# Closing the attention's pools and the first eight steps put into the attention's region of fixed order

## Chip, cores and metric

One core of a Trainium2 chip. The metric is the device time of one execution in microseconds (us); lower is better. Engines: TensorE (PE, its weight loads PEld), VectorE (DVE), ScalarE (ACT), GpSimd (POOL), and SyncE (SP), which issues the loads here.

## Reference

Three stages one behind the other, all in float32. A decaying linear attention over B=2, H=8, S=768, D=64 gives x (1536 x 512). It feeds two layers with d_ff = 2048, the first with an ELU, the second with a softplus.

```python
for b in range(nb):
    intra = einsum('bhic,bhjc->bhij', qb, kb) * Dmask
    intra = einsum('bhij,bhjd->bhid', intra, vb)
    inter = einsum('bhid,bhde->bhie', qb * lam_pow, kv_state)
    out[:, :, sl] = intra + inter
    kv_state = lam_block * kv_state + einsum('bhsd,bhse->bhde', kb * rev_pow, vb)
x = out as (tokens, heads * dim)
h = x @ w_in;   g = where(h > 0, h, exp(min(h, 0)) - 1);          x = g @ w_out
h = x @ w_in2;  g = maximum(h, 0) + log1p(exp(-abs(h)));          return g @ w_out2
```

## The kernel before

**Attention.** It runs over 12 chunks g of 128 tokens (6 for each of the two batches; state is carried inside a batch). For each chunk:
- S(g) is the scores on PE (att_s, L306, 8 matmuls a pair of banks, 16 rows in the trace), then the mask sc(g) on DVE (att_mask, L319, two instructions).
- X(g) is the chunk's output on PE (att_x): the part with the carried state first (L334, needs state(g-1) and the queries that POOL has scaled, L265), then the part inside the chunk (L343, needs sc(g)).
- T(g) is the state's product on PE (L370; it needs the keys that ACT, L284, and POOL, L291, have scaled). state(g) is formed from it on DVE (L376), and its decayed copy on POOL (L380).
- xh(g) on ACT (L357) and xl(g) on DVE (L358) split the chunk's output into a high and a low part, which the layers' matmuls read.

The program's order inside the loop is S(g+1), sc(g+1), scaling of chunk g+1, X(g), T(g), state(g), xh and xl(g). So PE has S(g+1) to do while the state of the chunk before is formed. Chunks 5 and 11 end a batch: they form no state, and chunk 6 needs none. There is no S(12).

**Weights.** Each weight is split on the chip into a high part wh and a low part wl. For the first five blocks fc of 128 rows this is done in halves (fc, i): i=0 for the first product, i=1 for the second. Such a half takes five steps (split_half), each on an in-order engine:
1. convert: two ACT instructions, r (L111) and c (L112), which read the loaded tile raw
2. shift: DVE, L116
3. round_up: DVE, L122
4. high: ACT, L125, writes wh
5. rest: DVE, L128, writes wl

The table PIECES lays the steps of (0, 0) and (1, 0) into chunks 5 to 11 of the attention: (1, 0) is converted behind chunk 8, shifted in chunk 9, rounded and made high in chunk 10, and its rest stands in chunk 11. The half (2, 0) and the later ones belong to early_step (table HALVES): (2, 0) to step 0, all five of its steps behind m1(0).

**Loads.** All loads but the constants go through SP's queue in the order of the table LOADS; the load of (2, 0) stands behind the last loads of the attention.

**Layers.** A step n is m1(n) on PE (12 matmuls of 128x512, L407 to L409), ACT's two instructions on its result (L418, L419), DVE's (L442), ACT's high part of g (L447), POOL's low part (L449), and two steps later m2(n-2) on PE (12 matmuls, L480). m1(0) needs (0, 0) and xh, xl of the first four chunks; m1(1) needs (1, 0); m1(2) needs (2, 0). The second loop of steps, from step 8, is unchanged by the diff.

**Order.** Inside `tc.manual_schedule()` every engine keeps the program's order. The kernel before has three such regions: the attention, steps 0 to 7, and (for all engines but DVE) the rest. Between the first two stands the closing of the attention's pools. Across two regions the scheduler may interleave.

```python
    with tc.manual_schedule():
        attention()
    close_attention()
    with tc.manual_schedule():
        for n in range(8):
            (early_step if n in HALVES else step)(n)
```

Of the kernel before, what the change touches and what calls it, by code (L numbers as in the profile page):

```python
# [48 lines left out]
def body(ctx, tc, consts, attqk, attkv, w1, w2, out):  # L49
# [480 lines left out]
    def close_attention():  # L530
        actx.close()
        late["acc"] = ctx.enter_context(tc.tile_pool(name="late", bufs=1, reuse_waits="tile"))
        late["tp"] = ctx.enter_context(tc.tile_pool(name="ltp", bufs=2, reuse_waits="tile"))
# [5 lines left out]
    def attention():  # L539
        setup()  # L540
        powers()
        decays()
        att_s(0)
        att_prep_k(0, att_turn_k())
        att_mask(0)
        for g in range(NCHUNK):
            before, behind = PIECES.get(g, ((), ()))
            att_s(g + 1)
            att_mask(g + 1)
            att_prep(g + 1)  # L550
            att_prep_k2(g + 1)
            if before:
                half(*before, 1 if g in (6, 9) else 2)
            ps = att_x(g)
            att_state(g)
            att_conv(g, ps)
            att_prep_k(g + 1)
            if behind:
                half(*behind, 1)
            loads(g or None)  # L560
# [43 lines left out]

    with tc.manual_schedule():
        attention()
    close_attention()
    with tc.manual_schedule():
        for n in range(8):
            (early_step if n in HALVES else step)(n)  # L610
    with tc.manual_schedule(engines={ET.PE, ET.Activation, ET.Pool, ET.SP}):
# [51 lines left out]
```

## Time and profile before

| what | value |
|---|---|
| time, median of 3 runs | 578.88 us (578.66 to 579.36) |
| profiled execution: its own time | 575.07 us |
| profiled execution: span of the core | 573.3 us |
| granted TensorE clock, mean | 0.999 |
| busy: PE / ACT / DVE / POOL | 563.6 / 361.3 / 341.7 / 165.3 us |

In the lists of instructions in order of time, a row gives start (us from the span's start), length (us), engine, line, operation, out<-in and, in brackets, how long the engine had stood idle before it and what ended that. One row can hold several instructions of a kind (x16); its length then runs from the first's start to the last's end. Matmuls are pipelined, so a row can begin a little before the row ahead of it ends.

### The profile page before, as it was taken

The page shows a single profiled execution, that of the slowest core. Times are in us where ns is not written, and L with a number is a line of the kernel's source. Part 1 is how long each engine was busy: PE and PEld are TensorE (multiplying, and loading weights), DVE is VectorE, ACT ScalarE, POOL GpSimd, SP SyncE. Part 2 cuts the span into 40 slices and gives each one's busy share as a digit, 9 for nine tenths or more (in the row PEclk, how much of TensorE's full clock was granted, in tenths as well). Part 3 has the DMA queues.
Part 4 walks back from the last instruction along what each step waited for, and adds up shares of the span by engine and source line. Part 5 has one row for each costly group of instructions (what it writes and reads, how often), then busy time and mean ns, then how long its engine had stood idle before and what let it go on. Part 6 is the DMA issues. An engine that isn't in the chain of part 4 may idle for free.

```text
span 573.3 us, 7779 instructions
## 1 busy us (share of the span) xinstructions
PE 563.6 (98%) x3031; PEld 468.6 (82%) x3031; DVE 341.7 (60%) x407; ACT 361.3 (63%) x597; POOL 165.3 (29%) x143
## 2 busy tenths in 40 slices
PE   9979999999999999999999999999999999999997
PEld 8867888888888888888888888888888888888885
DVE  6776644645454445113666967675799855656656
ACT  5566666666565654432877877756899755665562
POOL 4662221221222212432432452221221222222210
PEclk9999999999999999999999999999999999999999
DMA  8990321313322312000323202010241000100202
GB/s 334 408 405 19 147 74 74 146 74 105 117 74 90 131 73 74 0 2 0 120 109 141 73 1 73 18 57 1 74 148 73 2 0 1 73 1 0 74 0 75
DMA packets 10693, 49.60 MB, mean 87 GB/s; under 512 B 1184, under 2 KB 1568, under 8 KB 7072
## 3 DMA queue, kind: packets, MB, share of 16 engines
q1 hardware_dynamic: 10368, 48.89, 22.8%
q8 instruction: 24, 0.39, 0.3%
q10 hardware_dynamic: 288, 0.20, 0.1%
q14 instruction: 13, 0.11, 0.1%
HBM read 45.95 MB, written 3.15 MB: 86 GB/s over the span
## 4 chain that ended last, share of the span: by engine, by line
PE 91%; DMA 6%; DVE 1%; issue 0%; ACT 0%; SPq 0%; DVEq 0%; ACTq 0%
PE y L480 45%; PE hps L407 15%; PE hps L408 15%; PE hps L409 15%; DMA raw<-w 4%; DMA early<-attkv 2%; DMA kv<-attkv 1%; DVE yacc L527 0%; DVE sc L319 0%; PE xps L343 0%; SPq L250 0%; DVE state L376 0%; DVE c L122 0%; DVE yacc L482 0%; PE xps L334 0%
## 5 line engine op out<-in xcount | busy, mean ns | idle before, releaser
L407 PE MATMUL hps<-xh,wh 128*128 128x512 f32 x384 | 149.5, 389 | 0.0
L409 PE MATMUL hps<-xh,wl 128*128 128x512 f32 x384 | 149.5, 389 | 0.0
L408 PE MATMUL hps<-xl,wh 128*128 128x512 f32 x384 | 149.4, 389 | 0.0
L449 POOL TENSOR_TENSOR g<-v,g 128x512 fp32r<-128x512 f32 x48 | 62.9, 1310 | 193.1 <-ACT g L447 193.1
L480 PE MATMUL y<-g,wh 128*128 128x512 f32 x384 | 118.3, 389 | 0.0
L480 PE MATMUL y<-wh,g 128*128 128x512 f32 x382 | 117.7, 389 | 0.0
L449 POOL TENSOR_TENSOR g<-l,g 128x512 fp32r<-128x512 f32 x46 | 60.1, 1306 | 183.6 <-ACT g L447 164.2
L418 ACT ACTIVATE v<-hps 128x512 f32<-128x512 f32 x48 | 28.7, 598 | 100.4 <-PE hps L409 100.3
L442 DVE SCALAR_TENSOR_TENSOR v<-v,hps 128x512 f32<-128x512 f32 x48 | 32.9, 686 | 93.0 <-ACT v L419 92.8
L409 PEld LDWEIGHTS hps<-xh,wl 128*128 128x128 f32 x384 | 72.0, 188 | 15.1 <-DVE wl L128 0.2
L407 PEld LDWEIGHTS hps<-xh,wh 128*128 128x128 f32 x384 | 72.0, 188 | 15.1 <-issue 0.2
L408 PEld LDWEIGHTS hps<-xl,wh 128*128 128x128 f32 x384 | 72.1, 188 | 14.9
L480 PEld LDWEIGHTS y<-g,wh 128*128 128x128 f32 x384 | 72.1, 188 | 14.9
L480 PEld LDWEIGHTS y<-wh,g 128*128 128x128 f32 x382 | 71.7, 188 | 15.3 <-POOL g L449 0.2
L444 DVE TENSOR_TENSOR l<-l,u 128x512 f32<-128x512 f32 x48 | 75.6, 1574 | 4.4
L436 DVE SCALAR_TENSOR_TENSOR u<-u,e 128x512 f32<-128x512 f32 x48 | 33.6, 700 | 69.4 <-ACT l L430 69.4
L480 PE MATMUL y<-g,wl 128*128 128x512 f32 x192 | 74.7, 389 | 0.0
L480 PE MATMUL y<-wl,g 128*128 128x512 f32 x191 | 74.3, 389 | 0.0
L427 ACT ACTIVATE e<-hps 128x512 f32<-128x512 f32 x48 | 28.7, 598 | 71.2 <-PE hps L409 71.2
L128 DVE TENSOR_TENSOR wl<-c,wh 128x1024 fp32r<-128x1024 f32 (+1 forms) x36 | 50.0, 1389 | 14.4 <-ACT wh L125 14.0
L122 DVE CUSTOM_DVE_ANT_0 c<-r,c 128x2048 uint16<-128x2048 uint16 (+1 forms) x36 | 40.7, 1130 | 4.7 <-ACT c L112 1.8
L480 PEld LDWEIGHTS y<-g,wl 128*128 128x128 f32 x192 | 36.0, 188 | 7.6
(70 smaller groups left out, 605.7 us busy)
## 6 DMA issues: line engine op xcount, KB each, us to landing
raw<-w SPq DMA_DIRECT2D x28, 1024.0 KB, 4.8
early<-attkv SPq DMA_DIRECT2D x8, 512.0 KB, 10.2
raw<-w SPq DMA_DIRECT2D x8, 512.0 KB, 10.2
qk<-attqk SPq DMA_DIRECT2D x6, 512.0 KB, 8.1
early<-attqk SPq DMA_DIRECT2D x6, 512.0 KB, 10.8
out<-yacc SPq DMA_DIRECT2D x7, 256.0 KB, 2.0
kv<-attkv SPq DMA_DIRECT2D x3, 512.0 KB, 10.2
out<-o SPq DMA_DIRECT2D x4, 256.0 KB, 2.3
```

Of the source, the lines that this page charges most:

```text
L122: V.tensor_tensor(out=c, in0=r.bitcast(U32), in1=c, op=ALU.add)
L128: V.tensor_tensor(out=lo, in0=c.bitcast(F32), in1=hi.bitcast(F32), op=ALU.subtract)
L407: T.matmul(ps, wh[fc, 0][:, o], h[:, k, :], start=(k == 0), stop=False)
L408: T.matmul(ps, wh[fc, 0][:, o], l[:, k, :], start=False, stop=False)
L409: T.matmul(ps, wl[fc, 0][:, o], h[:, k, :], start=False, stop=(k == KD - 1))
L418: A.activation(out=v, in_=ps, func=AF.Relu, scale=-1.0)
L427: A.activation(out=e, in_=ps, func=AF.Abs)
L436: V.scalar_tensor_tensor(out=u, in0=u, scalar=-1.0, in1=e, op0=ALU.add, op1=ALU.subtract)
L442: V.scalar_tensor_tensor(out=v, in0=v, scalar=-1.0, in1=ps, op0=ALU.add, op1=ALU.max)
L444: V.tensor_tensor(out=v, in0=v, in1=u[0], op=ALU.subtract)
L449: eng.tensor_tensor(out=g[:, 1], in0=v, in1=g[:, 0].bitcast(F32), op=ALU.subtract)
L480: T.matmul(yps[m], a, b, start=(c == begin and i == 0), stop=(last and i == 2))
```

## The change

The two regions become one, with the closing of the pools inside it. No instruction is added or taken away; no size, tile or load changes.

```diff
     with tc.manual_schedule():
         attention()
-    close_attention()
-    with tc.manual_schedule():
+        close_attention()
         for n in range(8):
             (early_step if n in HALVES else step)(n)
```

What it moves is one half's split. On ACT, at the end of the attention, before the change (raw_133 and wh_757 are of the half (1, 0), raw and wh_847 of (2, 0); L357 is xh of the chunks, L284 the scaling of chunk 10's keys, L418 the first instruction on m1(0)'s result):

```order
L111 ACTIVATE r<-raw_133 128x512
L112 ACTIVATE c<-raw_133 128x512
L111 ACTIVATE r<-raw 128x512
L112 ACTIVATE c<-raw 128x512
L125 ACTIVATE wh_847<-r 128x512
L357 ACTIVATE xh_669<-xps 128x2x128 x2
L284 ACTIVATE early<-early,kdecay 128x64 x4
L125 ACTIVATE wh_757<-r 128x512
L357 ACTIVATE xh_669<-xps 128x2x128 x4
L418 ACTIVATE v<-hps 128x512
```

The same place with the change (wh_844 is now the high part of (2, 0)):

```order
L111 ACTIVATE r<-raw_133 128x512
L112 ACTIVATE c<-raw_133 128x512
L357 ACTIVATE xh_669<-xps 128x2x128 x2
L284 ACTIVATE early<-early,kdecay 128x64 x4
L125 ACTIVATE wh_757<-r 128x512
L357 ACTIVATE xh_669<-xps 128x2x128 x4
L111 ACTIVATE r<-raw 128x512
L112 ACTIVATE c<-raw 128x512
L125 ACTIVATE wh_844<-r 128x512
L418 ACTIVATE v<-hps 128x512
```

The three ACT instructions of (2, 0) stood ahead of xh(9), and now stand behind xh(11), the attention's last.

On DVE at the same place, before the change (wl_848 is the low part of (2, 0), wl_758 that of (1, 0); the first row holds the shifts of both halves, (1, 0) first; the three L358 rows are xl of chunks 9, 10 and 11, the two L376 rows state(9) and state(10), the L319 rows sc(11)):

```order
L116 TENSOR_SCALAR r<-r 128x512 x2
L122 ISA c<-r,c 128x1024
L376 TENSOR_TENSOR state<-stps,faded 128x256
L358 TENSOR_TENSOR xl_670<-xps,xh_669 128x2x128 x2
L128 TENSOR_TENSOR wl_848<-c,wh_847 128x512
L319 TENSOR_TENSOR sc<-sps_742,dmask 128x512
L319 TENSOR_TENSOR sc<-sps_743,dmask 128x512
L122 ISA c<-r,c 128x1024
L376 TENSOR_TENSOR state<-stps,faded 128x256
L358 TENSOR_TENSOR xl_670<-xps,xh_669 128x2x128 x2
L128 TENSOR_TENSOR wl_758<-c,wh_757 128x512
L358 TENSOR_TENSOR xl_670<-xps,xh_669 128x2x128 x2
```

With the change (the first L122 is that of (1, 0), the last that of (2, 0), whose L128 follows it):

```order
L116 TENSOR_SCALAR r<-r 128x512
L376 TENSOR_TENSOR state<-stps,faded 128x256
L358 TENSOR_TENSOR xl_670<-xps,xh_669 128x2x128 x2
L319 TENSOR_TENSOR sc<-sps_742,dmask 128x512
L319 TENSOR_TENSOR sc<-sps_743,dmask 128x512
L122 ISA c<-r,c 128x1024
L376 TENSOR_TENSOR state<-stps,faded 128x256
L358 TENSOR_TENSOR xl_670<-xps,xh_669 128x2x128 x2
L128 TENSOR_TENSOR wl_758<-c,wh_757 128x512
L358 TENSOR_TENSOR xl_670<-xps,xh_669 128x2x128 x2
L116 TENSOR_SCALAR r<-r 128x512
L122 ISA c<-r,c 128x1024
```

The three DVE instructions of (2, 0), which stood ahead of state(9) (shift and round_up) and ahead of sc(11) (rest), now follow xl(11). PE, POOL and SP keep their order; so do ACT and DVE from the first L442 on.

## Rows read from the trace of the kernel before

**Rows 1.** The page: busy time of each engine; the chain that ended last, by engine

```profile
PE 563.6 (98%) x3031; PEld 468.6 (82%) x3031; DVE 341.7 (60%) x407; ACT 361.3 (63%) x597; POOL 165.3 (29%) x143
...
PE 91%; DMA 6%; DVE 1%; issue 0%; ACT 0%; SPq 0%; DVEq 0%; ACTq 0%
```

**Rows 2.** The chain in order of time, 18 to 47 us: start, us, what

```profile
28.77 10.21 DMA raw<-w
...
40.95 0.42 DVE state L376
```

**Rows 3.** PE in order of time, 9 to 55 us

```profile
12.06 0.64 PE L370 MATMUL stps<-kv 128*64 128x64 f32 x16
...
36.42 0.64 PE L370 MATMUL stps<-kv 128*64 128x64 f32 x16
...
41.51 0.67 PE L334 MATMUL xps<-qk,state 64*64 64x128 f32 x16 [3.36 <-DVE state L376]
...
43.03 0.64 PE L370 MATMUL stps<-early 128*64 128x64 f32 x16
44.91 0.67 PE L334 MATMUL xps<-qk,state 64*64 64x128 f32 x16 [1.24 <-DVE state L376]
...
46.53 0.50 PE L407 MATMUL hps<-xh,wh 128*128 128x512 f32 x1
...
54.82 0.62 PE L480 MATMUL y<-g,wh 128*128 128x512 f32 x2
```

**Rows 4.** ACT in order of time, 35 to 50 us

```profile
35.61 0.69 ACT L112 ACTIVATE c<-raw 128x512 uint32<-128x512 uint32 x1
39.08 0.66 ACT L111 ACTIVATE r<-raw 128x512 f32<-128x512 f32 x1 [2.78 <-DMA raw<-w]
...
40.24 0.63 ACT L125 ACTIVATE wh<-r 128x512 fp32r<-128x512 f32 x1
...
46.64 0.66 ACT L357 ACTIVATE xh<-xps 128x256 fp32r<-128x256 f32 x2 [2.73 <-PE xps L343]
49.58 0.60 ACT L418 ACTIVATE v<-hps 128x512 f32<-128x512 f32 x1 [2.27 <-PE hps L409]
```

**Rows 5.** DVE in order of time, 12 to 54 us

```profile
12.84 0.42 DVE L376 TENSOR_TENSOR state<-stps,faded 128x256 f32<-128x256 f32 x1 [0.91 <-PE stps L370]
...
36.54 0.47 DVE L116 TENSOR_SCALAR r<-r 128x512 uint32<-128x512 uint32 x1
39.78 0.43 DVE L116 TENSOR_SCALAR r<-r 128x512 uint32<-128x512 uint32 x1 [2.77 <-ACT r L111]
...
42.54 1.28 DVE L319 TENSOR_TENSOR sc<-sps,dmask 128x512 f32<-128x512 f32 x2
43.74 0.68 DVE L122 CUSTOM_DVE_ANT_0 c<-r,c 128x1024 uint16<-128x1024 uint16 x1
...
45.34 0.68 DVE L128 TENSOR_TENSOR wl<-c,wh 128x512 fp32r<-128x512 f32 x1
47.06 0.76 DVE L358 TENSOR_TENSOR xl<-xps,xh 128x256 fp32r<-128x256 f32 x2 [1.04 <-ACT xh L357]
50.87 0.69 DVE L442 SCALAR_TENSOR_TENSOR v<-v,hps 128x512 f32<-128x512 f32 x1 [3.06 <-ACT v L419]
...
53.05 1.38 DVE L128 TENSOR_TENSOR wl<-c,wh 128x512 fp32r<-128x512 f32 x1 [0.33 <-ACT wh L125]
```

**Rows 6.** POOL in order of time, 35 to 53 us

```profile
35.44 1.28 POOL L265 TENSOR_TENSOR qk<-qk,qpow 128x512 f32<-128x512 f32 x1
...
41.44 0.62 POOL L380 TENSOR_TENSOR faded<-state,qpow 128x256 f32<-128x256 f32 x1 [3.96 <-DVE state L376]
...
52.57 1.31 POOL L449 TENSOR_TENSOR g<-v,g 128x512 fp32r<-128x512 f32 x1 [8.80 <-ACT g L447]
```

**Rows 7.** The page: loads by tile, count, KB each, median us from issue to landing

```profile
early<-attkv SPq DMA_DIRECT2D x8, 512.0 KB, 10.2
```

**Rows 8.** Busy time by stretch: PE, PEld, DVE, ACT, POOL; granted clock, DMA share, GB/s

```profile
50.00:60.00 10.00, 10.00 (x45) 8.11 (x45) 8.11 (x12) 9.90 (x19) 2.76 (x2) 1.00 0.13 39
```

## Prediction

> **What bounds the kernel now.** The page comes first: PE is busy for 563.6 of 573.3 us, and the chain that ended last lies on PE for 91% and on loads for 6% [rows 1]. So the end moves only by what PE loses, and PE's losses are few; the second view to read is PE in order of time. From the first m1 at 46.53 [rows 3] it runs matmul behind matmul, so whatever moves the start of m1(0) moves the end by as much, if nothing behind it opens a new gap. Ahead of m1(0) it stands idle twice, both times ended by DVE's state: 3.36 us before X(10), which starts at 41.51, and 1.24 us before X(11), which starts at 44.91 [rows 3].
>
> The third view, the chain in order of time, says why: the load of (2, 0) runs from 28.77 to 38.98, and from there the chain goes by ACT and DVE to state(9) at 40.95 [rows 2]. ACT had ended the conversion of (1, 0) at 36.30 (35.61 + 0.69) and then stood for 2.78 us at r of (2, 0), which waits for its load [rows 4]. DVE stood for 2.77 us at the shift of (2, 0), which waits for that r [rows 5]. Nothing of the attention needs this half. But xh(9) and the scaling of chunk 10's keys are queued behind it on ACT, and state(9), xl(9) and sc(11) on DVE, and state(9) is what X(10) waits for. A load that is wanted only by m1(2) holds up the attention through two in-order queues.
>
> **What the change moves.** It moves three ACT and three DVE instructions, the split of (2, 0), behind the attention's last xh and xl. It adds and removes none. The load itself keeps its place on SP, POOL and PE keep their order. I work out the new times in the profiled execution, first for what goes, then for what comes.
>
> *X(10).* S(11) ends on PE at 41.51 - 3.36 = 38.15 [rows 3]. T(9) ends at 36.42 + 0.64 = 37.06 [rows 3]; from a T's end to its state DVE takes 0.14 where it is free (T(1) ends at 12.06 + 0.64 = 12.70, state(1) starts at 12.84 [rows 3, 5]). DVE ends the shift of (1, 0) at 36.54 + 0.47 = 37.01 [rows 5]. So state(9) runs from 37.20 to 37.62, and 0.14 later (41.37 to 41.51 before [rows 2, 3]) X(10) could go: 37.76, earlier than PE is free. The whole 3.36 us goes; X(10) starts at 38.15.
>
> *X(11).* T(10) ends 2.16 us behind X(10)'s start (43.03 + 0.64 - 41.51 [rows 3]), at 40.31. state(10) can then start at 40.45, if DVE is free. Ahead of it there now stand xl(9) (0.76), sc(11) (1.28) and round_up of (1, 0) (0.68) [rows 5]; xl(9) needs xh(9), which ACT no longer holds back. From S(11)'s end, 38.15, and 0.1 for the signal: sc(11) to 39.53, round_up to 40.21. DVE is free 0.24 us before state(10). That is the tightest place of the sum. state(10) ends at 40.87, X(11) starts at 41.01. PE's gap ahead of it is 0.14 + 0.42 + 0.14 = 0.70 where it was 1.24, because there is no S(12) to fill it. This is what is late next. Gain: 3.36 + 0.54 = **3.90 us**.
>
> *What else X(10) and X(11) want.* The last load of the attention, chunk 11's keys and values, is issued ahead of the load of (2, 0), so before 28.77, and takes 10.2 us to land [rows 2, 7]: at 39.0 at the latest, 2 us before X(11). POOL's decayed copy of state(9) (0.62) and its scaling of chunk 11's queries (1.28) [rows 6] follow state(9)'s end and S(11)'s: they end at about 39.6, ahead of 41.01. ACT has xh(9) and the key scaling of chunk 10 done before T(10) can start. None of these is a new bound.
>
> *The split of (2, 0) in its new place.* Call the start of m1(0) zero; it is at 46.53 now [rows 3] and would be at 42.63. xh(11) ends at +0.77 (46.64 + 0.66), xl(11) at +1.29 (47.06 + 0.76) [rows 4, 5]. ACT converts: two instructions of up to 0.69 [rows 4], to about +2.0 as they overlap a little. DVE shifts (0.43) as soon as r and xl(11) are done, from +1.5 to +1.9, and rounds up behind c, 0.68, to +2.75. ACT makes the high part, 0.63, to +2.6. The rest takes DVE 0.68, at most 1.38 [rows 5], to between +3.45 and +4.15. Who wants these?
> - ACT: the first instruction on m1(0)'s result starts at +3.05 and had 2.27 us of idle time before it [rows 4]. The three instructions of (2, 0) end at +2.6. They fit, with 0.45 to spare.
> - DVE: L442 of step 0 starts at +4.34, after 3.06 us idle [rows 5]. It fits in either case.
> - PE: m1(2) starts at two thirds of the three m1 that end with the first L480 at 54.82 [rows 3]: (54.82 - 46.53) x 2/3 = +5.5. The high part is there 2.9 us earlier, the low part 1.35 at least.
>
> So the split is costed at nothing: idle ACT and DVE time during m1(0) hides it. If that cover were gone it would cost, at most, all of itself one behind the other: 0.66 + 0.69 + 0.43 + 0.68 + 0.63 + 1.38 = 4.47 us. The load of (2, 0) has landed at 39.0, 4 us before its new use, and even a late load would now hold up nothing of the attention.
>
> *Sum.* -3.90 + 0. The profiled execution would take 575.07 - 3.9 = 571.2 us. The median of the runs stands 3.81 above the profiled execution's time; I take the same gain from it: 578.88 - 3.9 = **575.0 us**. Bounds of the gain in the trace: below, 3.1, if DVE or POOL push state(10) back (next paragraph); above, 4.6, if no gap were left at all. How the loads stand in the runs without a profile no row tells. The loss before is tied to the landing of (2, 0) (X(10) started 2.5 us behind it), so if that comes later there by some time the gain grows by that time, and shrinks if it comes earlier.
>
> *A rule that speaks against it.* The row first: DVE's rest took 0.68 with POOL idle, and 1.38 where POOL's L449 ran beside it from 52.57, ending 0.55 behind POOL's end [rows 5, 6]. round_up of (1, 0) at 39.53 comes just as POOL's scaling of chunk 11's queries ends (about 39.6), so a lock could cost it some 0.1 us, which the 0.24 of slack takes. The Trainium skill, SBUF — State Buffer, section "Who interferes with whom", says that a VectorE instruction with two inputs in SBUF and a GpSimd instruction that reads SBUF exclude each other for their whole length. By that rule round_up, if POOL starts its 1.28 us shortly before it, is held until POOL ends; the trace agrees on the rest (1.38 against 0.68).
>
> **Rivals.**
> - *POOL holds round_up.* If POOL starts the scaling only at about 39.4 (it has to follow state(9) and the end of S(11)), it ends at 40.7; round_up ends 0.55 later, at 41.25, and state(10) slips from 40.45 to 41.25. The gain is 3.1: 575.8 us. For it: the order on POOL is fixed and it had 3.96 us of waiting at this place [rows 6]. Against: by the sum it starts at 38.3. Chance 7%.
> - *Nothing is won in the runs* (the change does what it says, and it doesn't count). If in executions without a profile (2, 0) lands before ACT is through with (1, 0), at 36.3, there is no stall to remove, and only the 0.5 before X(11) is left: 578.4 us. For it: the runs differ from the profile by 3.81 us that no row explains. Against: loads run one behind the other up to there, and this one would have to land 2.7 us earlier in an execution that is longer on the whole. Chance 6%.
> - *More is won.* The 3.81 us lie partly in the loads, and the stall before was longer by 1.5 us or more: 573.5 or less. Chance 9%.
> - *Slower: the split lies on PE's path.* Place: ACT between xh(11) and the first instruction on m1(0)'s result. ACT is 9.90 of 10 us busy from 50 to 60 [rows 8], so what overruns its 2.27 us of idle time passes into step 1 and on to m1(2). Price: the 4.47 us of the split, all uncovered, and behind it the two instructions on m1(0)'s result, 1.2, which g(0) and so m2(0) wait for: 5.7 - 3.9 = +1.8, or 580.7 us. It decides against the change from the point where the low part of (2, 0) comes over 3.9 us behind m1(2)'s need, after +9.4, where I have +4.15 at most. Chance 2%.
>
> **How the numbers follow.** The forecast, a gain of 3.9 give or take half a microsecond, has 76%. Predicted: 575.0 us. The range reaches down to 573.4, for loads that are later in the runs by up to 1.6, and up to 576.4: past the 575.8 of POOL's hold, with 0.6 for a stall that is a little shorter without a profile. Left out are the case without a gain, the slower one and half of "more is won", together some 13%. A measurement of this kernel can tell about 0.2%, 1.2 us. Faster by more than that: the forecast, POOL's hold and "more is won", 92%. Within it: the case without a gain, 6%. Slower: 2%.
>
> **What would show it.** In the profile after, PE should have no wait before X(10), one of about 0.7 before X(11), and m1(0) at 42.6. ACT's wait for the load of (2, 0) should be gone, and its r should start within 0.1 of xh(11)'s end. L418 of step 0 should start 3.05 behind m1(0), as before. The forecast is wrong if PE waits at m1(2) for wl, if L418 is later than that, or if X(11) waits for POOL or for a load; and if the span falls by 3.9 but the runs don't, the stall was the profile's own.

## The result

| | before | after |
|---|---|---|
| runs, median | 578.10 us (575.56 to 579.36, 6 runs) | 571.44 us (571.08 to 573.32, 6 runs) |
| profiled execution | 575.07 us | 571.56 us |
| its span | 573.3 us | 569.4 us |

The ratio of the runs is 0.9898, 95% interval 0.9871 to 0.9924: faster by about 1.0%. In the profile the span fell by 3.9 us, as forecast. The runs fell by 6.7, to below the range of 573.4 to 576.4.

The page of the changed kernel, busy time and chain, beside [rows 1]:

```profile
PE 563.9 (99%) x3031; PEld 468.9 (82%) x3031; DVE 341.8 (60%) x407; ACT 361.2 (63%) x597; POOL 164.8 (29%) x143
...
PE 98%; DVE 1%; DMA 0%; issue 0%; DVEq 0%
```

The loads' 6% of the chain are gone. PE, ACT and DVE in order of time, beside [rows 3], [rows 4] and [rows 5]:

```profile
37.26 1.16 PE L306 MATMUL sps<-qk 64*128 64x128 f32 x16
38.35 0.67 PE L334 MATMUL xps<-qk,state 64*64 64x128 f32 x16
...
41.20 0.67 PE L334 MATMUL xps<-qk,state 64*64 64x128 f32 x16 [0.69 <-DVE state L376]
...
42.82 0.50 PE L407 MATMUL hps<-xh,wh 128*128 128x512 f32 x1
```

```profile
36.91 0.66 ACT L357 ACTIVATE xh<-xps 128x256 fp32r<-128x256 f32 x2 [0.36 <-PE xps L343]
...
43.48 0.68 ACT L111 ACTIVATE r<-raw 128x512 f32<-128x512 f32 x1
...
45.89 0.60 ACT L418 ACTIVATE v<-hps 128x512 f32<-128x512 f32 x1 [0.61 <-PE hps L409]
```

```profile
39.66 0.71 DVE L122 CUSTOM_DVE_ANT_0 c<-r,c 128x1024 uint16<-128x1024 uint16 x1
40.62 0.42 DVE L376 TENSOR_TENSOR state<-stps,faded 128x256 f32<-128x256 f32 x1 [0.26 <-PE stps L370]
...
45.55 0.69 DVE L128 TENSOR_TENSOR wl<-c,wh 128x512 fp32r<-128x512 f32 x1
```

X(10) follows S(11) with no wait, X(11) waits 0.69, m1(0) starts 3.7 us earlier than before, with the attention 0.3 late in this execution. The split of (2, 0) starts as xh(11) ends and is through at 46.24, 3.4 us behind m1(0)'s start, where m1(2) starts 5.6 behind it, at 48.41; ACT still waits for PE before L418. So the trace holds no surprise. The question is what the other 2.8 us in the runs were: 6.7 - 3.9. Six runs a side are few for that figure: beside 19 and 23 further runs of the kernel before, whose medians are 576.69 and 576.55, the gain of the change is 5.6 and 5.2 us (after_later and after_again below).

### The profile page after: what moved, and what is told of

Read it like the earlier page. It is cut to its first block, busy times and chain, and to the rows that moved or that the text cites. A ratio compares the mean times of both kernels' runs of the same rounds, so it can differ in the third digit from the quotient of the medians.

```text
span 569.4 us, 7780 instructions
## 1 busy us (share of the span) xinstructions
PE 563.9 (99%) x3031; PEld 468.9 (82%) x3031; DVE 341.8 (60%) x407; ACT 361.2 (63%) x597; POOL 164.8 (29%) x143
## 4 chain that ended last, share of the span: by engine, by line
PE 98%; DVE 1%; DMA 0%; issue 0%; DVEq 0%
PE y L480 45%; PE hps L407 15%; PE hps L409 15%; PE hps L408 15%; PE sps L306 2%; PE xps L343 2%; PE xps L334 1%; PE stps L370 1%; DMA const_t<-consts 0%; DVE dmask L211 0%; DVE yacc L527 0%; DVE yacc L482 0%; PE kps L272 0%; DVE state L376 0%; DVE yacc L519 0%
## 5 line engine op out<-in xcount | busy, mean ns | idle before, releaser
L480 PE MATMUL y<-g,wh 128*128 128x512 f32 x384 | 118.1, 389 | 0.0
L480 PE MATMUL y<-wh,g 128*128 128x512 f32 x382 | 117.7, 389 | 0.0
L418 ACT ACTIVATE v<-hps 128x512 f32<-128x512 f32 x48 | 28.7, 597 | 98.8 <-PE hps L409 98.7
L442 DVE SCALAR_TENSOR_TENSOR v<-v,hps 128x512 f32<-128x512 f32 x48 | 33.0, 687 | 90.8 <-ACT v L419 90.7
L480 PEld LDWEIGHTS y<-wh,g 128*128 128x128 f32 x382 | 71.7, 188 | 15.4 <-POOL g L449 0.2
L480 PEld LDWEIGHTS y<-g,wh 128*128 128x128 f32 x384 | 72.0, 188 | 14.9
L480 PE MATMUL y<-g,wl 128*128 128x512 f32 x192 | 74.7, 389 | 0.0
L480 PE MATMUL y<-wl,g 128*128 128x512 f32 x191 | 74.3, 389 | 0.0
L128 DVE TENSOR_TENSOR wl<-c,wh 128x1024 fp32r<-128x1024 f32 (+1 forms) x36 | 50.1, 1392 | 14.5 <-ACT wh L125 13.9
L122 DVE CUSTOM_DVE_ANT_0 c<-r,c 128x2048 uint16<-128x2048 uint16 (+1 forms) x36 | 40.7, 1130 | 4.7 <-ACT c L112 1.8
L480 PEld LDWEIGHTS y<-g,wl 128*128 128x128 f32 x192 | 36.1, 188 | 7.6
```

The source lines that it names most:

```text
L122: V.tensor_tensor(out=c, in0=r.bitcast(U32), in1=c, op=ALU.add)
L128: V.tensor_tensor(out=lo, in0=c.bitcast(F32), in1=hi.bitcast(F32), op=ALU.subtract)
L418: A.activation(out=v, in_=ps, func=AF.Relu, scale=-1.0)
L442: V.scalar_tensor_tensor(out=v, in0=v, scalar=-1.0, in1=ps, op0=ALU.add, op1=ALU.max)
L480: T.matmul(yps[m], a, b, start=(c == begin and i == 0), stop=(last and i == 2))
```

## The experiments

At first there were two theories. A: in most executions the load of (2, 0) lands later than in the profiled one, so the stall is longer. B: the runs lose their time elsewhere. Beside the first four kernels 19 runs of the kernel before were timed; they took 575.71 to 579.66, median 576.69.

**placed.** The one region, with the split of (2, 0) written where it stood before.

```diff
                 half(*before, 1 if g in (6, 9) else 2)
+            if g == 9:
+                half(2, 0, 4)
             ps = att_x(g)
             att_state(g)
             att_conv(g, ps)
             att_prep_k(g + 1)
+            if g == 9:
+                half(2, 0, 1)
```

> The one region of the change, with the five steps of (2, 0) written at the places that they had before (convert, shift, round_up and high in chunk 9 ahead of X(9), rest behind xl(9)), so that every engine has the order of the kernel before. Both theories: the time of the kernel before, profile about 575.1 and runs 575.5 to 579.4; the region itself costs or gives nothing. If it comes out near 571.4, the order is not what counts.

Measured: 577.07 us (575.61 to 578.6, 10 runs), ratio to before 0.9991 (0.9970 to 1.0011). So the order is all that the change does, as far as these runs can tell (0.3%). This time the profiled execution was a longer one, 575.6 of span, and its stretches show what the first profile did not. Busy time by stretch as in [rows 8] (behind the last bracket: granted clock, DMA share, GB/s), first the kernel before, then placed:

```profile
42.00:44.00 2.00, 1.67 (x40) 1.42 (x32) 2.00 (x5) 1.54 (x5) 1.77 (x2) 1.00 0.72 289
...
46.00:48.00 2.00, 2.00 (x18) 1.59 (x15) 0.77 (x3) 0.66 (x2) 0.00 (x0) 1.00 0.03 8
```

```profile
40.00:42.00 2.00, 0.32 (x12) 0.35 (x16) 1.86 (x5) 2.00 (x7) 0.39 (x1) 1.00 1.02 397
42.00:44.00 2.00, 2.00 (x45) 1.83 (x36) 2.00 (x5) 1.48 (x6) 1.93 (x2) 0.77 0.80 322
44.00:46.00 2.00, 1.31 (x24) 0.96 (x20) 2.00 (x5) 0.23 (x1) 0.00 (x0) 0.50 0.15 61
46.00:48.00 2.00, 2.00 (x20) 1.57 (x16) 0.19 (x1) 0.00 (x0) 0.00 (x0) 0.50 0.03 8
...
50.00:52.00 2.00, 2.00 (x11) 1.62 (x10) 0.00 (x0) 0.04 (x1) 0.00 (x0) 1.00 0.00 0
```

The granted clock, 1.00 in the first profile until after PE's last matmul, falls to 0.50 here (1.2 instead of 2.4 GHz). The average of 0.77 from 42 to 44 puts the fall at about 43.1, some 1.4 us after PE came back from its stall; the clock stays at half until about 50. PE and the chain of that execution:

```profile
41.68 0.67 PE L334 MATMUL xps<-qk,state 64*64 64x128 f32 x16 [3.45 <-DVE state L376]
...
45.08 1.13 PE L334 MATMUL xps<-qk,state 64*64 64x128 f32 x16 [0.69 <-DVE state L376]
46.14 1.97 PE L343 MATMUL xps<-sc,early 128*64 128x128 f32 x16
48.04 0.80 PE L407 MATMUL hps<-xh,wh 128*128 128x512 f32 x1
...
57.20 0.62 PE L480 MATMUL y<-g,wh 128*128 128x512 f32 x2
```

```profile
28.81 10.34 DMA raw<-w
39.25 0.66 ACT r L111
```

The load of (2, 0) landed at 39.15, 0.17 later than in the first profile. X(10) is late by just that. But X(11)'s first part takes 1.13 us where it took 0.67 at full clock [rows 3], and the first L480 comes at 57.20, 2.38 behind [rows 3]. So a third theory, C: the stall itself puts PE's clock down in most executions, and the work after it runs at half speed for some us.

**nowait.** As placed, but the split of (2, 0) reads the loaded words of (1, 0).

```diff
-        convert(whalf.pop((fc, i)), r, c)
+        convert(whalf[(1, 0) if (fc, i) == (2, 0) else (fc, i)], r, c)
```

> As placed, but the split of (2, 0) reads the loaded words of (1, 0), so it waits for no late load (the weights of half (2, 0) are thus those of (1, 0)). Theory A (the stall ends with the landing of (2, 0), and in most timed executions of the kernel before that comes later than in the profiled one): X(10) no longer waits for a load, but DVE's shift, round_up and rest still stand ahead of state(9) and sc(11), so X(11) starts some 1.3 us later than in the changed kernel; profile 572.9, runs 572.4 to 574.8, without values of 577 and more. Theory B (the 3 us by which timed executions of before exceed its profile are lost elsewhere, and not to this load): the runs go down by what the profile does, 2.2, to about 575.5 to 577.2.

Measured: 573.07 us (572.64 to 573.41, 4 runs), 0.9925 (0.9898 to 0.9952); span 570.8, clock 1.00 in all four. Without the wait for the load the spread is gone as well. What is left over the changed kernel's span, 1.4, is the price of the instructions of (2, 0) that still stand ahead of state(9) and state(10): PE waits twice for DVE, 2.2 us in all and 1.2 at most, where the changed kernel waits 0.69.

```profile
PE xps L334 <- DVE state L376: 2.2, 2, 1.2
```

**later.** As placed, the load of (2, 0) one place further back.

```diff
-    ... ("w", 2, 0), ("w", 0, 1)),
+    ... ("w", 0, 1), ("w", 2, 0)),
```

> As placed, with the load of (2, 0) one place later on SP's queue (behind that of (0, 1), 512 KB, about 1.28 us). Theory A: X(10) starts 1.3 us later; profile 576.4, runs about 1.3 above the kernel before. Theory B, or a stall that is not the load's: no change.

Measured: 579.35 us (577.7 to 581.33, 10 runs), 1.0037 (1.0017 to 1.0056). The chain, PE's wait and one stretch:

```profile
30.07 10.24 DMA raw<-w
```

```profile
42.84 1.13 PE L334 MATMUL xps<-qk,state 64*64 64x128 f32 x16 [4.61 <-DVE state L376]
```

```profile
40.00:42.00 2.00, 0.00 (x0) 0.00 (x0) 0.76 (x2) 1.58 (x3) 0.00 (x0) 0.53 1.01 389
```

The landing moved by 1.2 us, and so did X(10). The runs grew by more, 2.3 over placed and 2.7 over the kernel before, where 1.3 was expected. In this execution the clock fell while PE still stood, and X(10) itself ran at half clock (1.13 instead of 0.67 us for the same matmuls). Six of the ten runs had a mean clock of 0.990 or 0.991, in placed three of ten.

**after_later.** The changed kernel with the same edit.

> The changed kernel with the load of (2, 0) one place later, as in the run labelled later. Theory A: the half is not wanted before 43.5, its load lands at about 40.5; no change, profile 571.5, runs 571.1 to 573.3. If the load still counted, +1.3.

Measured: 571.10 us (571.02 to 571.82, 4 runs). The change took the load off the path.

Theory A foresaw the times of nowait and after_later, but for a reason that placed's profile does not bear out: the load landed only 0.17 later there. What tells C from A is a stall without a load, and a stall in which PE has work. Beside the next four kernels 23 runs of the kernel before were timed; they took 575.19 to 580.14, median 576.55.

**fill.** As placed, with matmuls of zeros behind S(11).

```diff
             att_s(g + 1)
+            if g == 10:
+                warm(14)
```

> As placed (the order of the kernel before), with 14 matmuls of zeros (128x128, into a bank that nobody reads until it is written anew) behind S(11) on PE, so that PE works for some 3.0 of the 3.4 us in which it stands before X(10). Nothing else waits for them. Theory C (PE's stall before X(10) lowers the granted clock to half for some us in most executions, and that is what the runs of before have over its profile): the stall stays, X(10) at 41.5, but the clock stays at 1.00; runs 575.1 to 575.9, without the values from 576.2 to 579.7. Theory B (the clock falls, or the time is lost, for a reason that is not PE standing idle there): runs as the kernel before, 575.7 to 579.7.

Measured: 575.24 us (575.04 to 575.41, 12 runs), 0.9971 (0.9958 to 0.9984); clock 0.998 to 1.000 in all twelve.

```profile
38.27 3.39 PE L201 MATMUL warm<-const-float32-0.0 128*128 128x128 f32 x28
41.70 0.67 PE L334 MATMUL xps<-qk,state 64*64 64x128 f32 x16
```

The matmuls of zeros fill PE's whole wait. X(10) starts as late as in placed, at 41.70, and ACT waits for the load as there. Yet the spread, 5 us in the kernel before, has shrunk to 0.4, and every run stands at or below the lower end of its range. Work that nobody reads made the kernel faster by 1.3 us in the median.

**gap.** The changed kernel, with DVE kept busy ahead of state(9).

```diff
             ps = att_x(g)
+            if g == 9:
+                idle = ac.tile([P, 2, P], F32, name="idle")
+                for i in range(11):
+                    V.tensor_tensor(out=idle, in0=dmask[:, 0, :2], in1=qpow[:, :2], op=ALU.mult)
             att_state(g)
```

> The changed kernel with eleven multiplications of 128x256 on DVE ahead of state(9), some 4 us, whose result nobody reads: state(9) comes as late as in the kernel before, but no load is waited for. Theory C: PE stands 3.4 us before X(10) as in before, and the clock falls as there; profile 575 to 577, runs 575.3 to 579, spread over more than 2 us. Theory A (the loss in the runs is the load's): the runs come out at the stall alone, 571.4 + 3.7 = 575.1, spread below 1 us.

Measured: 577.39 us (577.1 to 579.98, 10 runs), 1.0021 (1.0003 to 1.0039). The eleven took 5.43 us, more than I had counted on, so the stall is 4.42 long, not 3.4. X(10) starts 4.6 later than in the changed kernel (42.95 against 38.35), so theory A would now give 571.4 + 4.6 = 576.0; every run lies above that.

```profile
42.95 1.13 PE L334 MATMUL xps<-qk,state 64*64 64x128 f32 x16 [4.42 <-DVE state L376]
```

```profile
40.00:42.00 2.00, 0.00 (x0) 0.00 (x0) 1.86 (x5) 0.00 (x0) 0.00 (x0) 0.65 1.01 393
42.00:44.00 2.00, 1.05 (x16) 0.76 (x16) 1.97 (x7) 0.00 (x0) 1.12 (x2) 0.50 0.75 303
44.00:46.00 2.00, 2.00 (x26) 1.99 (x24) 1.28 (x3) 0.00 (x0) 0.73 (x1) 0.50 0.11 43
```

No load is waited for here, and the clock falls all the same, in each of the ten runs (0.991 to 0.997).

The 42 runs of the kernel before (19 and 23), by the mean granted clock of the execution:

```
mean clock        runs    us                   span
0.999 to 1.000     5      575.19 to 575.72     573.4 to 573.7
0.996 to 0.998    23      575.71 to 577.25     573.9 to 575.2
0.993 to 0.994     3      577.32 to 577.83     575.5 to 576.0
0.990 to 0.991    11      578.36 to 580.14     576.6 to 578.4
```

From row to row the time follows the clock. Inside a row the times still spread by up to 1.8 us, in part because the time less the span varies from 1.7 to 3.0 us; that part is not explained. The profile that stood ahead of the prediction was one of the few executions in which the clock did not fall while PE had work, as in the top row.

**first and after_again.** The wait that is left, 0.69 us before X(11), can be filled with m1(0), which needs nothing of chunks 9 to 11.

```diff
+            if g == NCHUNK - 1:
+                first = m1(0)
+                half(2, 0, 5)
             ps = att_x(g)
             att_state(g)
+            if g == NCHUNK - 1:
+                pointwise1(0, first)
             att_conv(g, ps)
...
-        ps = m1(n)
+        ps = m1(n) if n else None
...
-        pointwise1(n, ps)
+        if n:
+            pointwise1(n, ps)
```

> The changed kernel with m1(0) ahead of X(11) on PE, the split of (2, 0) behind xl(10), and the two ACT instructions on m1(0)'s result ahead of xh(11): m1(0) wants nothing of chunks 9 to 11, so it fills the 0.69 us in which PE waits for state(10). X(11) then has its state long before. Profile 571.56 - 0.7 = 570.9, runs 570.4 to 570.7. If ACT or DVE come late for m1(2) or m2(0) in the new order, 571.5 or more.

> The changed kernel once more, beside the others of this call: 571.0 to 571.8 for most runs, clock 1.00; no theory has the clock fall here, since PE stands for 0.7 us at most.

Measured: first 570.89 us (570.45 to 570.96, 4 runs), the changed kernel again 571.35 us (571.22 to 571.85, 5 runs), 0.9899 and 0.9910 of before. PE has no wait left between S(11) and the layers:

```profile
40.28 0.64 PE L370 MATMUL stps<-early 128*64 128x64 f32 x16
40.85 0.50 PE L407 MATMUL hps<-xh,wh 128*128 128x512 f32 x1
...
43.80 0.67 PE L334 MATMUL xps<-qk,state 64*64 64x128 f32 x16
```

That is 0.46 us better than the change in the medians, where 0.7 was expected. Every run of the one lies below every run of the other, though the intervals of their ratios overlap, so the sign is plain and the size is not. In its profile S(11) started 0.41 later than in that of the changed kernel (37.67 against 37.26), for a reason ahead of the edit, and the span is 0.2 shorter all the same (569.2 against 569.4): 0.6 together.

## Why the prediction was right and wrong

**The stall and its cause: right.** nowait took the load away and left the places: 2.5 of the 3.9 us of span are the wait for (2, 0), the other 1.4 the DVE instructions in front of the states.

**X(10), X(11) and the gap of 0.70: right.** 0.69 was measured, no wait before X(10), and m1(0) at 42.82 against 42.63, with S(11) 0.27 later than in the first profile (37.26 against 36.99). The profiled execution came to 571.56 for a forecast 571.2.

**The split of (2, 0) at no cost: right.** L418 came 3.07 behind m1(0) (45.89 - 42.82), as before the change, and PE has no wait at m1(2).

**The port: right, and small.** round_up took 0.71 and ended at 40.37, 0.55 behind POOL's end at 39.82 (38.54 + 1.28), as far behind it as DVE's rest was in [rows 5, 6]. It cost 0.03 us over the 0.68 of [rows 5]; state(10) still waited for PE. The Trainium skill, SBUF — State Buffer, section "Who interferes with whom", says that a VectorE instruction with two inputs in SBUF and a GpSimd instruction that reads SBUF exclude each other; the trace fits that.

**The step that failed** is "I take the same gain from it", the step from the profiled execution to the median of the runs. It costed the stall at its own length alone, and carried the 3.81 us by which the runs stood above the profile over to the changed kernel unchanged. There they were gone: its median, 571.44, is its profiled execution's 571.56. In most executions the stall has a second price: PE's clock falls to half, and the work that follows pays. The prediction says of the 3.81 us that "no row explains" them, and it gave a gain from them 9%, by later loads. The landing of placed, 0.17 later in an execution that was 2.3 longer, speaks against later loads; fill, which keeps the load and X(10)'s late start and loses the excess, shows the clock. Without the clock the forecast's own arithmetic holds: fill's 575.24 to 571.35 of the changed kernel is 3.9.

The forecast's 575.0 and the measured 571.44 lie 3.6 us apart. Of these, 1.3 is what the clock costs in a typical execution (576.55 of the kernel before against fill's 575.24). The other 2.3 comes from the start: the forecast set out from 578.88, the median of three runs, where 23 later runs had 576.55. All three, 578.66 to 579.36, lie in the range of the bottom row of the table, which holds 11 of 42 runs. Their own clock is not on record, so it is not shown that the clock made them slow, nor why all three were.

The Trainium skill tells of such a price, and I left it out: TensorE: Matmul & The Clock Gate, section "HAM oscillation — how this bites in real kernels", says of a loop that waits for loads that a wait which is long enough puts PE's clock back, so that the next work starts at half rate. The runs agree in part. With stalls of 3.4 to 4.6 us the mean clock was below 0.999 in most executions or all: in 37 of 42 of the kernel before, 9 of 10 of placed, and all ten each of later and gap. Where PE waited at most 1.24 us (nowait, fill, the changed kernel) it was 0.999 or more, but for one run of fill at 0.998 that was no slower than the others. The next work, though, did not always start at half rate: in placed X(10) still took 0.67 us, and the clock fell 1.4 us later. I had read the granted clock of 1.00 in the profile as the kernel's, where it was one execution's; a median 0.66% above the profiled time was the sign that the profile was not the usual case.

**What stays open:** two of the six runs of the changed kernel took 573.2 and 573.3, with spans of 571.4 and 571.5, at a mean clock of 0.999, which a run of 571.1 had too, so the clock does not explain them. None of the nine later runs of it and of after_later did so, and no trace of such a run is at hand.

## What to carry to other kernels

Work that nobody needs soon must not stand ahead of the critical chain in an in-order queue, least of all if it waits for a load: here three ACT and three DVE instructions of a later weight held up the attention. A stall of several us on TensorE (3.4 to 4.6 here) can cost more than its length, because the clock may fall in it or behind it; if such a stall can't be removed, matmuls of zeros in it may pay, as they did in fill. Where the runs stand above the profiled execution by more than their own spread, compare clock and span of each run before carrying a gain from the one to the other, and take more than three runs for the start.

## What the runs showed of the hardware that was not expected

- One and the same stall costs a different amount from execution to execution: the 42 runs of the kernel before took 575.19 to 580.14 us. In placed's profile the clock fell about 1.4 us after PE had gone back to work. In later's and gap's it fell some 2 us into the stall, at about 40.1 and 40.6 (estimates from the averages 0.53 and 0.65 of the stretch from 40 to 42), so part of the slow stretch passed while PE stood. That is how later's execution with its stall of 4.61 us had nearly the span of placed's with 3.45, 575.8 and 575.6.
- Matmuls of zeros that nobody reads kept the clock at 0.998 or more in fill.
- At the very start the profile of the kernel before gives a clock of 1.00, but 16 rows of the same matmuls of zeros took 3.75 us there (0.23 each), and 28 of them 3.39 us in fill (0.12 each). So they ran at about half speed at the start, whatever the records grant.
